# Ring of five 32 KB slots in place of nine of 16 KB, and the last output weights in three loads

## The chip, the cores and the metric

The kernel runs on one core of a Trainium2 chip. The metric is the device time of one execution in microseconds (us). Instructions run on TensorE (PE; its weight loads are listed as PEld), VectorE (DVE), ScalarE (ACT) and GpSimd (POOL). SyncE (SP) only issues transfers here; 16 DMA engines carry them out.

## The reference

One token passes through two blocks, and a gate mixes them. Block A is attention of 32 query heads over 4 groups of cached keys and values, 65536 positions of 128 numbers each; block B is a gated MLP. All inputs are bfloat16.

```python
q = (x @ wq).reshape(B, Sq, Hq, Dh)                  # 1 token, D = 1024, Hq = 32, Dh = 128
scores = einsum(q, k) * Dh ** -0.5                   # Hkv = 4, Sk = 65536, 8 heads share a group
a = (softmax(scores) @ v).reshape(1, Hq * Dh) @ wo
z = gelu(x @ w_in)                                   # D x 3584
z1, z2 = z[:1792], layernorm(z[1792:])
b = (z1 * (w_sp * z2 + b_sp)) @ w_out                # w_sp is 1 x 1
g = sigmoid((x * gate_w).sum())
out = g * a + (1 - g) * b
```

Keys and values are 4 x 65536 x 128 x 2 bytes each, 67.1 MB; with the weights the kernel reads 162.01 MB once.

## The kernel before

**Units.** A group's 65536 positions are cut in 8 units of 8192 positions (UK = 128 x 64). A unit of keys or values is one load of 2 MB: each of the 128 partitions receives 64 consecutive positions of 128 numbers, 16 KB in one run (`kv`). There are 32 key units and 32 value units.

**Ring.** All large loads go in one list, `stream`, in the order of their use: four loads of wq, then for each of the first eight steps a unit of keys, with one of four loads of w_in (steps 0 to 3) or one of two of w_out (steps 5 and 7), then keys and values in turn, and last four loads of wo. Load n goes to slot n modulo NS of a ring in SBUF (L323 issues it on SP). It waits until PE has finished with the load that held the slot before. The order in SP's queue is that of the list, and `issue` puts a load at the place of the program where its slot has been used up.

**Steps.** At step n PE works on key unit n and on value unit n - 9 (`k_piece`, `s_piece`, `pt_piece`, `pv_piece`).
- Keys: a unit goes in four pieces of 16 transposes (L388, 128 x 128 by an identity). Results lie in four PSUM banks; DVE (L396) or ACT (L393) copies them to one of NKTS key buffers. One piece later, four matmuls (L410) make scores from them.
- After the fourth piece DVE copies the unit's scores to one of NSC score buffers and takes their maximum (L415). When a group's eight units are done, its maximum is known.
- Values: ACT takes the exponentials of a unit's scores (L436), PE transposes them (L443), DVE copies them (L446), and 16 matmuls (L455) multiply them with the value unit. At the end of a group `out_piece` scales the sums and puts them into `ovec`.

**Around it.** At the start ACT issues four small loads: x, gate_w, w_sp and b_sp (`small`, L261). x and gate_w come as runs of two numbers, 4 bytes. PE's first instruction is a matmul for the gate (L348), which needs x and gate_w; the 256 matmuls with wq follow (L363). `win_piece` runs 56 matmuls (L503) for each of the four loads of w_in, with a weight operand whose 128 columns lie 7 numbers apart; after the fourth the mixer's chain of small operations runs, for which PE waits (L524, L529). `wout_piece` (L551) follows. At the end 32 matmuls for each load of wo (L598), one DVE addition (L604) and the output's transfer (L607).

Of the kernel before, what the change touches and what calls it, by code (L numbers as in the profile page):

```python
# [137 lines left out]
def bass_gated_mix__gqa_block_cached__mixer_gmlp__decode_kernel(  # L138
# [25 lines left out]
    TILES = 64  # L164
    UK = 128 * TILES
    NU = Sk // UK
    NS = 9
    SLOT = 8192
    NB = TILES // 8
    NKTS = 8  # L170
    NSC = 12
    QW = DO // 4
    SCALE = 1.0 / math.sqrt(Dh)
    GELU_C = 0.044715
# [52 lines left out]
    def slot(n):  # L227
        return ab("RING", SLOT, (n % NS) * SLOT)

# [14 lines left out]
    def B(i):  # L244
        return ("bank", i)
# [12 lines left out]
    def small(dst, src, key):  # L258
        def f(e):
            with nc.allow_non_contiguous_dma(reason="a few bytes"):  # L260
                return e.dma_start(dst, src)  # L261
        P("ACT", f, w=[key], dma=key)

    small(vw(xT, 0, [[2, 4], [1, 2]]), A_x[0, 0].rearrange("(i p k) -> p i k", i=4, k=2), "xT")
    small(vw(gw, 0, [[2, 4], [1, 2]]), gate_w.rearrange("(i p k) -> p i k", i=4, k=2), "gw")
    small(wb[:, 0:1], bass.AP(tensor=B_w_sp.tensor, offset=B_w_sp.offset, ap=[[0, 128], [1, 1]]), "wsp")
    small(wb[:, 1:2], bass.AP(tensor=B_b_sp.tensor, offset=B_b_sp.offset, ap=[[0, 128], [1, 1]]), "bsp")


    stream = []  # L270
    place = {}

    def load(key, src, n):
        place[key] = len(stream)
        stream.append((key, src, n))

    def rows(w, i, c):

# [1 line left out]

    WQ_N = HQ * Dh

    def kv(cache, g, u):
        return cache[0, g, UK * u:UK * (u + 1), :].rearrange("(p x) d -> p (x d)", p=128)

    KV = [(g, u) for g in range(G) for u in range(NU)]
    for i in range(4):
        load(("wq", i), rows(A_wq, i, 2), 2 * WQ_N)
    steps = []
    for n in range(NU):  # L290
        load(("k", n), kv(A_k_cache, *KV[n]), SLOT)
        aux = None
        if n < 4:
            load(("win", n), rows(B_w_in, n, 2), 2 * F)
            aux = ("win", n)
        elif n in (5, 7):
            i = (n - 5) // 2
            load(("wout", i), rows(B_w_out, i, 7), 7 * DO)
            aux = ("wout", i)
        steps.append((n, None, aux))  # L300
    total = G * NU
    for n in range(NU, total + NU + 1):
        k = n if n < total else None
        v = n - NU - 1
        if k is not None:
            load(("k", k), kv(A_k_cache, *KV[k]), SLOT)
        if v >= 0:
            load(("v", v), kv(A_v_cache, *KV[v]), SLOT)
        else:
            v = None  # L310
        steps.append((k, v, None))
    for i in range(4):
        load(("wo", i), rows(A_wo, i, 8), 8 * DO)

    issued = [0]

    def issue(upto):
        while issued[0] < min(upto, len(stream)):
            n = issued[0]
            assert n < NS or stream[n - NS][0] in used  # L320
            key, src, ln = stream[n]
            s = n % NS
            P("SP", lambda e, n=n, src=src, ln=ln: e.dma_start(slot(n)[:, 0:ln], src), w=[("slot", s)], dma="s%d" % s)  # L323
            issued[0] += 1

    used = set()

    def use(key):
        issue(place[key] + 1)
        used.add(key)  # L330
        return slot(place[key]), ("slot", place[key] % NS)

    issue(NS)

# [22 lines left out]
    for i in range(4):  # L357
        sl, key = use(("wq", i))

        def f(e, i=i, sl=sl):  # L360
            for k in range(2):
                for h in range(HQ):
                    ins = e.matmul(pf(OB)[:, h:h + 1], sl[:, WQ_N * k + 128 * h:WQ_N * k + 128 * (h + 1)],  # L363
                                   xT[:, 2 * i + k:2 * i + k + 1], start=(i == 0 and k == 0 and h == 0),
                                   stop=(i == 3 and k == 1), skip_group_check=True)
            return ins
        P("PE", f, r=["xT", key], w=[B(OB)])
        issue(place[("wq", i)] + NS + 1)
    for g in range(G):
        P("DVE", lambda e, g=g: e.tensor_copy(vw(qpad, 128 * g, [[40, 4], [1, 8]]),  # L370
                                              vw(pf(OB), 8 * g, [[0, 4], [1, 8]])),
# [6 lines left out]
    def k_piece(n, j):  # L378
        sl, key = use(("k", n))
        first = nbatch[0]  # L380
        for b in (2 * j, 2 * j + 1):
            i = nbatch[0]
            nbatch[0] += 1
            pb = KTB[i % 4]

            def tr(e, b=b, pb=pb):
                for t in range(8):
                    ins = e.transpose(pbf(pb)[:, 128 * t:128 * (t + 1)],  # L388
                                      sl[:, 128 * (8 * b + t):128 * (8 * b + t + 1)], idb)
                return ins  # L390
            P("PE", tr, r=["idb", key], w=[B(pb)])
            if b in (2, 5, 7):
                P("ACT", lambda e, i=i, pb=pb: e.activation(ktb(i), pbf(pb), ACTF.Copy),  # L393
                  w=[("kt", i % NKTS), B(pb)])
            else:
                P("DVE", lambda e, i=i, pb=pb: e.tensor_copy(ktb(i), pbf(pb)), w=[("kt", i % NKTS), B(pb)])  # L396
        if j == 3:
            issue(place[("k", n)] + NS + 1)
        pend.append((n, j, first))

    def s_piece():
# [46 lines left out]
    def pv_piece(n):  # L448
        g, u = KV[n]
        sl, key = use(("v", n))  # L450

        def f(e):
            for xi in range(4):
                for cg in range(4):
                    ins = e.matmul(pf(OB)[32 * cg:32 * (cg + 1), :],  # L455
                                   ptsb(n)[:, 128 * xi + 32 * cg:128 * xi + 32 * (cg + 1)],
                                   vw(sl, 128 * (4 * cg + xi), [[2048, 4], [1, 128]]),
                                   start=(u == 0 and xi == 0), stop=(u == NU - 1 and xi == 3),
                                   tile_position=(0, 32 * cg), skip_group_check=True)
            return ins  # L460
        P("PE", f, r=[("ptsb", n % 2), key], w=[B(OB)])
        issue(place[("v", n)] + NS + 1)
        if u == NU - 1:
            out_piece(g)

# [30 lines left out]
    def win_piece(i):  # L496
        sl, key = use(("win", i))

        def f(e):
            for k in range(2):  # L500
                for z in range(2 * FC):
                    c0 = F * k + FH * (z // FC) + 128 * 7 * (z % FC // 7) + z % 7
                    ins = e.matmul(pf(MB)[:, z:z + 1], vw(sl, c0, [[7, 128]]), xT[:, 2 * i + k:2 * i + k + 1],  # L503
                                   start=(i == 0 and k == 0 and z == 0), stop=(i == 3 and k == 1),
                                   skip_group_check=True)
            return ins
        P("PE", f, r=["xT", key], w=[B(MB)])
        issue(place[("win", i)] + NS + 1)
        if i == 3:
            mixer_piece()  # L510

# [33 lines left out]
    def wout_piece(i):  # L545
        sl, key = use(("wout", i))

        def f(e):
            for c in range(7):
                for q in range(4):  # L550
                    ins = e.matmul(pf(MB)[32 * q:32 * q + 1, 0:QW], yb[:, 7 * i + c:7 * i + c + 1],  # L551
                                   sl[:, DO * c + QW * q:DO * c + QW * (q + 1)],
                                   start=(i == 0 and c == 0), stop=(i == 1 and c == 6), tile_position=(0, 32 * q),
                                   skip_group_check=True)
            return ins
        P("PE", f, r=["yb", key], w=[B(MB)])
        issue(place[("wout", i)] + NS + 1)
        if i == 1:
            P("ACT", lambda e: e.activation(brow[0:97, :], pf(MB)[0:97, 0:QW], ACTF.Copy), w=["brow", B(MB)])

# [8 lines left out]
    for si, (k, v, aux) in enumerate(steps):  # L569
# [14 lines left out]
                pv_piece(v)  # L584
        if v is not None and v % NU == 0:
            weight_piece(v // NU)
        if aux is not None:
            (win_piece if aux[0] == "win" else wout_piece)(aux[1])


    FB = KTB[0]
    for i in range(4):
        sl, key = use(("wo", i))

        def f(e, i=i, sl=sl):
            for c in range(8):
                for q in range(4):
                    ins = e.matmul(pf(FB)[32 * q:32 * q + 1, 0:QW], ovec[:, 8 * i + c:8 * i + c + 1],  # L598
                                   sl[:, DO * c + QW * q:DO * c + QW * (q + 1)],
                                   start=(i == 0 and c == 0), stop=(i == 3 and c == 7), tile_position=(0, 32 * q),  # L600
                                   skip_group_check=True)
            return ins
        P("PE", f, r=[("ovec", i), key], w=[B(FB)])
    P("DVE", lambda e: e.tensor_tensor(orow[0:97, :], pf(FB)[0:97, 0:QW], brow[0:97, :], ALU.add),  # L604
      r=["brow"], w=["orow", B(FB)])
    osrc = bass.AP(tensor=arena, offset=OFF["OROW"], ap=[[32 * NA, 4], [1, QW]])
# [31 lines left out]
```

## Time and profile before

| | us |
|---|---|
| median of 8 runs (lowest, highest) | 395.24 (394.88, 395.69) |
| the profiled execution | 395.69 |
| its span, first to last instruction | 393.2 |
| PE busy | 275.0 (70%) |
| DVE busy | 160.3 (41%) |
| ACT busy | 124.3 (32%) |
| first matmul starts | 41.01 |
| last matmul of wo starts its group | 388.74 |

The span is read as 40 equal slices of 9.8 us. Each row of the second part of the profile gives an engine's busy share in tenths, and a last row the bytes moved per second. Queue q1 is SP's, with all large loads; q10 is ACT's, with the four small ones; q8 and q14 carry instructions. A wait is named after what ended it: "PE <- DMA" means that PE stood until a transfer had landed.

### The profile page before, as it was taken

Reading aid. Unit: us, or ns where it says so; the run is one execution under the profiler, and the core shown is the slowest. Engines: PE = TensorE matmul, PEld = TensorE weight load, DVE = VectorE, ACT = ScalarE, POOL = GpSimd, SP = SyncE. Lnnn points to the kernel's source line nnn. Section 1 sums busy time; section 2 is a strip of 40 time slices with the busy share of each in tenths; the row PEclk is TensorE's granted clock in tenths of the full one; section 3 lists DMA queues with packets and bytes.
Section 4 is the critical chain, followed back from the end, with each engine's and each line's share of the span. In section 5 each row is a group of like instructions: output and inputs, shape, how many; then the busy total and the mean of one; then the engine's idle time right before and its main releaser. Section 6 shows DMA issues by size and latency. Waiting matters only on the chain.

```text
span 393.2 us, 8544 instructions
## 1 busy us (share of the span) xinstructions
PE 275.0 (70%) x3902; PEld 194.6 (49%) x3902; DVE 160.3 (41%) x347; ACT 124.3 (32%) x171; POOL 1.5 (0%) x8
## 2 busy tenths in 40 slices
PE   0000699996998999997957687679767775644543
PEld 0000688885776666665645455457545553211121
DVE  2000044346666666676535345366434454200200
ACT  1000033333556555553614234235233334210000
POOL 1000000000000000000000000000000000000000
PEclk9999998986999999998989889689888898555555
DMA  8999999999999999999999999999999999999992
GB/s 315 405 418 422 421 428 431 427 422 424 425 422 430 423 430 425 427 427 426 425 427 427 427 425 423 425 427 428 428 430 427 424 428 423 430 424 425 432 395 89
DMA packets 12619, 162.55 MB, mean 413 GB/s; under 512 B 2596, under 2 KB 2600, under 8 KB 2600
## 3 DMA queue, kind: packets, MB, share of 16 engines
q1 hardware_dynamic: 11240, 162.01, 97.3%
q8 instruction: 30, 0.49, 0.5%
q10 hardware_dynamic: 1344, 0.00, 0.2%
q14 instruction: 5, 0.04, 0.0%
HBM read 162.01 MB, written 0.00 MB: 412 GB/s over the span
## 4 chain that ended last, share of the span: by engine, by line
DMA 60%; PE 30%; DVE 7%; ACT 1%; issue 1%; ACTq 0%; DVEq 0%
DMA arena<-in_A_k_cache_dram 30%; PE pb L388 16%; DMA arena<-in_A_wo_dram 11%; DMA arena<-in_gate_w_dram 10%; DMA arena<-in_A_v_cache_dram 10%; PE pb L410 5%; DVE arena L396 4%; PE pb L503 3%; PE pb L455 2%; PE pb L363 2%; DVE arena L415 2%; PE pb L443 1%; ACT arena L393 0%; PE pb L598 0%; PE pb L551 0%
## 5 line engine op out<-in xcount | busy, mean ns | idle before, releaser
L388 PE MATMUL pb<-arena 128*128 128x128 bf16 x2048 | 153.9, 235 | 27.7 <-DMA arena<-in_A_k_cache_dram 27.6
L388 PEld LDWEIGHTS pb<-arena 128*128 128x128 bf16 x2048 | 132.6, 106 | 56.1 <-DMA arena<-in_A_k_cache_dram 33.1
L396 DVE COPY arena<-pb 128x1024 bf16<-128x1024 bf16 x160 | 108.4, 690 | 110.5 <-PE pb L388 109.7
L393 ACT ACTIVATE arena<-pb 128x1024 bf16<-128x1024 bf16 x96 | 97.9, 1020 | 161.3 <-PE pb L388 161.3
L410 PE MATMUL pb<-arena 128*32 128x512 bf16 x512 | 54.8, 418 | 5.7 <-DVE arena L415 3.8
L455 PE MATMUL pb<-arena 128*32 128x512 bf16 x512 | 40.1, 441 | 19.4 <-DMA arena<-in_A_v_cache_dram 18.7
L455 PEld LDWEIGHTS pb<-arena 128*32 128x32 bf16 x512 | 14.2, 104 | 33.3 <-issue 22.5
L348 PE MATMUL pb<-arena 128*128 128x1 f32 x2 | 0.6, 361 | 41.0 <-DVE arena L347 41.0
L436 ACT ACTIVATE arena<-arena 128x512 bf16<-128x512 f32 x32 | 22.8, 713 | 16.3 <-PE pb L443 14.5
L446 DVE COPY arena<-pb 128x512 bf16<-128x512 bf16 x32 | 13.6, 424 | 29.7 <-PE pb L443 29.7
L410 PEld LDWEIGHTS pb<-arena 128*32 128x32 bf16 x512 | 13.3, 93 | 22.1 <-DVE arena L415 7.0
L415 DVE TENSOR_SCALAR_CACHE_REDUCE arena<-pb 128x512 f32<-128x512 f32 x32 | 21.8, 682 | 2.8 <-PE pb L410 2.8
L348 PEld LDWEIGHTS pb<-arena 128*128 128x128 f32 x2 | 0.5, 309 | 41.0 <-DVE arena L347 41.0
L346 DVE TENSOR_TENSOR arena<-arena 128x8 f32<-128x8 bf16 x1 | 0.2, 166 | 37.2 <-DMA arena<-in_gate_w_dram 37.2
L443 PE MATMUL pb<-arena 128*128 128x128 bf16 x128 | 15.1, 253 | 0.0
L443 PEld LDWEIGHTS pb<-arena 128*128 128x128 bf16 x128 | 8.9, 112 | 11.3 <-issue 11.3
L598 PE MATMUL pb<-arena 128*1 128x256 bf16 x128 | 7.5, 413 | 8.8 <-DMA arena<-in_A_wo_dram 8.8
L503 PEld LDWEIGHTS pb<-arena 128*128 128x128 bf16 x224 | 12.3, 153 | 0.9 <-issue 0.9
L503 PE MATMUL pb<-arena 128*128 128x1 bf16 x224 | 12.6, 192 | 0.0
L350 ACT ACTIVATE arena<-pb 128x1 f32<-128x1 f32 x1 | 0.2, 171 | 34.7 <-PE pb L348 34.7
L598 PEld LDWEIGHTS pb<-arena 128*1 128x1 bf16 x128 | 3.8, 115 | 12.2 <-DMA arena<-in_A_wo_dram 6.7
L363 PE MATMUL pb<-arena 128*128 128x1 bf16 x256 | 7.1, 165 | 1.5 <-issue 1.5
(78 smaller groups left out, 60.5 us busy)
## 6 DMA issues: line engine op xcount, KB each, us to landing
arena<-in_A_k_cache_dram SPq DMA_DIRECT2D x32, 2048.0 KB, 29.5
arena<-in_A_v_cache_dram SPq DMA_DIRECT2D x32, 2048.0 KB, 37.3
arena<-in_A_wq_dram SPq DMA_DIRECT2D x4, 2048.0 KB, 14.6
arena<-in_A_wo_dram SPq DMA_DIRECT2D x4, 2048.0 KB, 42.0
arena<-in_B_w_in_dram SPq DMA_DIRECT2D x4, 1792.0 KB, 22.6
arena<-in_B_w_out_dram SPq DMA_DIRECT2D x2, 1792.0 KB, 15.9
arena<-in_A_x_dram ACTq DMA_DIRECT2D x1, 2.0 KB, 22.3
arena<-in_gate_w_dram ACTq DMA_DIRECT2D x1, 2.0 KB, 39.3
```

Source lines behind the costliest of these rows:

```text
L363: ins = e.matmul(pf(OB)[:, h:h + 1], sl[:, WQ_N * k + 128 * h:WQ_N * k + 128 * (h + 1)], xT[:, 2 * i + k:2 * i + k + 1], start=(i == 0 and ...
L388: ins = e.transpose(pbf(pb)[:, 128 * t:128 * (t + 1)], sl[:, 128 * (8 * b + t):128 * (8 * b + t + 1)], idb)
L393: P("ACT", lambda e, i=i, pb=pb: e.activation(ktb(i), pbf(pb), ACTF.Copy), w=[("kt", i % NKTS), B(pb)])
L396: P("DVE", lambda e, i=i, pb=pb: e.tensor_copy(ktb(i), pbf(pb)), w=[("kt", i % NKTS), B(pb)])
L410: ins = e.matmul(pf(SCB)[32 * cg:32 * (cg + 1), :], qpad[:, 128 * g + 32 * j:128 * g + 32 * (j + 1)], src, start=(j == 0), stop=(j == 3), ...
L415: P("DVE", lambda e: e.tensor_scalar(scs(n), pf(SCB), 0.0, None, op0=ALU.add, op1=ALU.max, accum_out=maxc[:, n:n + 1]), w=[("sc", n % NSC) ...
L436: P("ACT", lambda e: e.activation(psb(n), scs(n), ACTF.Exp, bias=gcol(g, K_NB), scale=SCALE, accum_out=lp[:, n:n + 1]), r=[("sc", n % NSC) ...
L443: ins = e.transpose(pbf(PTB)[:, 128 * xi:128 * (xi + 1)], psb(n)[:, 128 * xi:128 * (xi + 1)], idb)
L446: P("DVE", lambda e: e.tensor_copy(ptsb(n), pbf(PTB)[:, 0:512]), w=[("ptsb", n % 2), B(PTB)])
L455: ins = e.matmul(pf(OB)[32 * cg:32 * (cg + 1), :], ptsb(n)[:, 128 * xi + 32 * cg:128 * xi + 32 * (cg + 1)], vw(sl, 128 * (4 * cg + xi), [[ ...
L503: ins = e.matmul(pf(MB)[:, z:z + 1], vw(sl, c0, [[7, 128]]), xT[:, 2 * i + k:2 * i + k + 1], start=(i == 0 and k == 0 and z == 0), stop=(i ...
L598: ins = e.matmul(pf(FB)[32 * q:32 * q + 1, 0:QW], ovec[:, 8 * i + c:8 * i + c + 1], sl[:, DO * c + QW * q:DO * c + QW * (q + 1)], start=(i ...
```

## The change

- The ring has five slots of 32 KB per partition in place of nine of 16 KB. A load brings two units: keys n and n + 1, values n and n + 1, two loads of wq or w_in, or both of w_out. A partition receives 128 consecutive positions of keys, 32 KB in one run (28 KB for w_in and w_out). The slot is free when PE has finished with the second unit (`done`).
- The rows of wq, w_in and w_out are dealt to the partitions in blocks of 4 and 14 in place of 2 and 7, and x and gate_w to match, in runs of 8 bytes.
- The weight operand of L503 has its columns 14 numbers apart in place of 7. The two w_in units of a load are used one after the other, after steps 1 and 3; both w_out units after step 6.
- wo comes in six loads: three of 2 MB as before, and the fourth in pieces of 4, 2 and 2 of its 8 rows per partition, with 16, 8 and 8 matmuls.
- Key buffers (NKTS) go from 8 to 6 and score buffers (NSC) from 12 to 10.

```diff
-    NS = 9
-    SLOT = 8192
+    NS = 5
+    SLOT = 16384
     NB = TILES // 8
-    NKTS = 8
-    NSC = 12
+    NKTS = 6
+    NSC = 10
...
-    small(vw(xT, 0, [[2, 4], [1, 2]]), A_x[0, 0].rearrange("(i p k) -> p i k", i=4, k=2), "xT")
-    small(vw(gw, 0, [[2, 4], [1, 2]]), gate_w.rearrange("(i p k) -> p i k", i=4, k=2), "gw")
+    small(vw(xT, 0, [[4, 2], [1, 4]]), A_x[0, 0].rearrange("(i p k) -> p i k", i=2, k=4), "xT")
+    small(vw(gw, 0, [[4, 2], [1, 4]]), gate_w.rearrange("(i p k) -> p i k", i=2, k=4), "gw")
...
+    def kv(cache, n):
+        g, u = KV[n]
+        return cache[0, g, UK * u:UK * (u + 2), :].rearrange("(p x) d -> p (x d)", p=128)
+
+    def pair(name, cache, n):
+        load([(name, n), (name, n + 1)], [(0, kv(cache, n))])
...
+    for i in range(0, 4, 2):
+        load([("wq", i), ("wq", i + 1)], [(0, rows(A_wq, i // 2, 4))])
     steps = []
     for n in range(NU):
+        if n % 2 == 0:
+            pair("k", A_k_cache, n)
+        aux = ()
+        if n in (1, 3):
+            load([("win", n - 1), ("win", n)], [(0, rows(B_w_in, n // 2, 4))])
+            aux = (("win", n - 1), ("win", n))
+        elif n == 5:
+            load([("wout", 0), ("wout", 1)], [(0, rows(B_w_out, 0, 14))])
+        elif n == 6:
+            aux = (("wout", 0), ("wout", 1))
...
+    WO = [(0, 0, 8), (1, 0, 8), (2, 0, 8), (3, 0, 4), (3, 4, 6), (3, 6, 8)]
+    for i, c0, c1 in WO:
+        load([("wo", i, c0)], [(0, rows(A_wo, i, 8)[:, DO * c0:DO * c1])])
...
+    def done(key):
+        n = place[key][0]
+        if key == stream[n][0][-1]:
+            issue(n + NS + 1)
...
-                    c0 = F * k + FH * (z // FC) + 128 * 7 * (z % FC // 7) + z % 7
-                    ins = e.matmul(pf(MB)[:, z:z + 1], vw(sl, c0, [[7, 128]]), xT[:, 2 * i + k:2 * i + k + 1],
+                    c0 = F * k + FH * (z // FC) + z % FC
+                    ins = e.matmul(pf(MB)[:, z:z + 1], vw(sl, c0, [[FC, 128]]), xT[:, 2 * i + k:2 * i + k + 1],
...
-    for i in range(4):
-        sl, key = use(("wo", i))
+    for i, c0, c1 in WO:
+        sl, key = use(("wo", i, c0))
...
+            for c in range(c0, c1):
                 for q in range(4):
+                    o = DO * (c - c0) + QW * q
...
+                                   sl[:, o:o + QW], start=(i == 0 and c == 0), stop=(i == 3 and c == 7),
```

More of the change, by code (lines that the diff above doesn't have):

```diff
@@ L271, in bass_gated_mix__gqa_block_cached__mixer_gmlp__decode_kernel, with load @@
     place = {}
-    def load(key, src, n):
-        place[key] = len(stream)
-        stream.append((key, src, n))
+    def load(keys, pieces):
+        for i, key in enumerate(keys):
+            place[key] = (len(stream), i)
+        stream.append((keys, pieces))
     def rows(w, i, c):
@@ L281, in bass_gated_mix__gqa_block_cached__mixer_gmlp__decode_kernel @@
     WQ_N = HQ * Dh
-    def kv(cache, g, u):
-        return cache[0, g, UK * u:UK * (u + 1), :].rearrange("(p x) d -> p (x d)", p=128)
+    def kv(cache, n):
[3 more added lines that the diff above has]
+        load([(name, n), (name, n + 1)], [(0, kv(cache, n))])
     KV = [(g, u) for g in range(G) for u in range(NU)]
-    for i in range(4):
-        load(("wq", i), rows(A_wq, i, 2), 2 * WQ_N)
+    total = G * NU
+    for i in range(0, 4, 2):
+        load([("wq", i), ("wq", i + 1)], [(0, rows(A_wq, i // 2, 4))])
     steps = []
     for n in range(NU):
[L291 to L299, printed above, removed]
+        if n % 2 == 0:
[8 more added lines that the diff above has]
+            aux = (("wout", 0), ("wout", 1))
         steps.append((n, None, aux))
-    total = G * NU
     for n in range(NU, total + NU + 1):
@@ L304, in bass_gated_mix__gqa_block_cached__mixer_gmlp__decode_kernel @@
         v = n - NU - 1
-        if k is not None:
-            load(("k", k), kv(A_k_cache, *KV[k]), SLOT)
+        if k is not None and k % 2 == 0:
+            pair("k", A_k_cache, k)
         if v >= 0:
-            load(("v", v), kv(A_v_cache, *KV[v]), SLOT)
+            if v % 2 == 0:
+                pair("v", A_v_cache, v)
         else:
             v = None
-        steps.append((k, v, None))
-    for i in range(4):
-        load(("wo", i), rows(A_wo, i, 8), 8 * DO)
+        steps.append((k, v, ()))
+    WO = [(0, 0, 8), (1, 0, 8), (2, 0, 8), (3, 0, 4), (3, 4, 6), (3, 6, 8)]
+    for i, c0, c1 in WO:
+        load([("wo", i, c0)], [(0, rows(A_wo, i, 8)[:, DO * c0:DO * c1])])
+    WIDTH = {"wq": 2 * WQ_N, "win": 2 * F, "wout": 7 * DO, "wo": 8 * DO, "k": UK, "v": UK}
     issued = [0]
+    used = set()
     def issue(upto):
@@ L319, in issue, with f @@
             n = issued[0]
-            assert n < NS or stream[n - NS][0] in used
-            key, src, ln = stream[n]
+            assert n < NS or all(k in used for k in stream[n - NS][0])
+            keys, pieces = stream[n]
             s = n % NS
-            P("SP", lambda e, n=n, src=src, ln=ln: e.dma_start(slot(n)[:, 0:ln], src), w=[("slot", s)], dma="s%d" % s)
+            def f(e, n=n, pieces=pieces):
+                for c0, src in pieces:
+                    ins = e.dma_start(slot(n)[:, c0:c0 + src.shape[1]], src)
+                return ins
+            P("SP", f, w=[("slot", s)], dma="s%d" % s)
             issued[0] += 1
-    used = set()
     def use(key):
-        issue(place[key] + 1)
+        n, i = place[key]
+        issue(n + 1)
         used.add(key)
-        return slot(place[key]), ("slot", place[key] % NS)
+        w = WIDTH[key[0]]
+        return slot(n)[:, i * w:(i + 1) * w], ("slot", n % NS)
+    def done(key):
+        n = place[key][0]
+        if key == stream[n][0][-1]:
+            issue(n + NS + 1)
     issue(NS)
@@ L367, in bass_gated_mix__gqa_block_cached__mixer_gmlp__decode_kernel @@
         P("PE", f, r=["xT", key], w=[B(OB)])
-        issue(place[("wq", i)] + NS + 1)
+        done(("wq", i))
     for g in range(G):
@@ L397, in k_piece @@
         if j == 3:
-            issue(place[("k", n)] + NS + 1)
+            done(("k", n))
         pend.append((n, j, first))
@@ L461, in pv_piece @@
         P("PE", f, r=[("ptsb", n % 2), key], w=[B(OB)])
-        issue(place[("v", n)] + NS + 1)
+        done(("v", n))
         if u == NU - 1:
@@ L507, in win_piece @@
         P("PE", f, r=["xT", key], w=[B(MB)])
-        issue(place[("win", i)] + NS + 1)
+        done(("win", i))
         if i == 3:
@@ L556, in wout_piece @@
         P("PE", f, r=["yb", key], w=[B(MB)])
-        issue(place[("wout", i)] + NS + 1)
+        done(("wout", i))
         if i == 1:
@@ L586, in bass_gated_mix__gqa_block_cached__mixer_gmlp__decode_kernel, with f @@
             weight_piece(v // NU)
-        if aux is not None:
-            (win_piece if aux[0] == "win" else wout_piece)(aux[1])
+        for a in aux:
+            (win_piece if a[0] == "win" else wout_piece)(a[1])
     FB = KTB[0]
-    for i in range(4):
-        sl, key = use(("wo", i))
-        def f(e, i=i, sl=sl):
-            for c in range(8):
+    for i, c0, c1 in WO:
+        sl, key = use(("wo", i, c0))
+        def f(e, i=i, sl=sl, c0=c0, c1=c1):
+            for c in range(c0, c1):
                 for q in range(4):
+                    o = DO * (c - c0) + QW * q
                     ins = e.matmul(pf(FB)[32 * q:32 * q + 1, 0:QW], ovec[:, 8 * i + c:8 * i + c + 1],
-                                   sl[:, DO * c + QW * q:DO * c + QW * (q + 1)],
-                                   start=(i == 0 and c == 0), stop=(i == 3 and c == 7), tile_position=(0, 32 * q),
-                                   skip_group_check=True)
+                                   sl[:, o:o + QW], start=(i == 0 and c == 0), stop=(i == 3 and c == 7),
+                                   tile_position=(0, 32 * q), skip_group_check=True)
             return ins
         P("PE", f, r=[("ovec", i), key], w=[B(FB)])
+        done(("wo", i, c0))
     P("DVE", lambda e: e.tensor_tensor(orow[0:97, :], pf(FB)[0:97, 0:QW], brow[0:97, :], ALU.add),
```

## The prediction

> **What bounds the kernel now.** I read the page from its second part down: slices, queues, then the waits, the stretches and the last microseconds.
>
> ```profile
> span 393.2 us, 8544 instructions
> DMA  8999999999999999999999999999999999999992
> GB/s 315 405 418 422 421 428 431 427 422 424 425 422 430 423 430 425 427 427 426 425 427 427 427 425 423 425 427 428 428 430 427 424 428 423 430 424 425 432 395 89
> q1 hardware_dynamic: 11240, 162.01, 97.3%
> q10 hardware_dynamic: 1344, 0.00, 0.2%
> ```
>
> The reader is to see that the DMA engines are full in every slice but the first and the last, and that one queue, q1 (SP's loads), is 97.3% of it. The rate is flat near 426 GB/s. q10 holds ACT's four small loads: 1344 packets in 0.2% of 16 x 393.2 us, so 9.4 ns for a packet of a few bytes.
>
> ```profile
> DMA to landing us min/median/max: 7.8/36.1/43.3
> PE pb L388 <- DMA arena<-in_A_k_cache_dram: 27.6, 12, 4.0
> PE pb L455 <- DMA arena<-in_A_v_cache_dram: 18.7, 9, 2.5
> SPq L323 <- PE pb L388: 221.7, 32, 10.5
> ```
>
> The shortest time from issue to landing is 7.8 us, while a 2 MB load alone takes 2097 KB / 426 GB/s = 4.92 us: no load was issued to an empty queue. PE waits for keys and values; SP waits for PE to free slots. So the time is bytes over rate, plus the start, plus what follows the last landing.
>
> The stretches (columns: PE, PEld, DVE, ACT and POOL busy, clock, DMA share, GB/s) show where PE has no slack:
>
> ```profile
> 42.00:50.00 8.00, 6.48 (x243) 6.42 (x241) 0.32 (x2) 0.00 (x0) 0.00 (x0) 1.00 1.02 423
> 50.00:88.00 38.00, 37.79 (x541) 31.84 (x538) 15.86 (x30) 12.28 (x12) 0.00 (x0) 0.91 1.00 425
> 160.00:250.00 90.00, 70.61 (x992) 49.79 (x988) 45.97 (x93) 36.80 (x51) 0.00 (x0) 0.92 1.01 426
> 250.00:340.00 90.00, 68.94 (x868) 48.01 (x872) 43.53 (x95) 32.58 (x50) 0.00 (x0) 0.82 1.01 426
> ```
>
> From 50 to 88 us PE is busy 37.79 of 38 us and works off a backlog; the ring hides that. From 160 us it idles a fifth. The tail, from the timeline:
>
> ```profile
> 388.74 1.87 PE L598 MATMUL pb<-arena 128*1 128x256 bf16 x32 [3.07 <-DMA arena<-in_A_wo_dram]
> 390.67 0.42 DVE L604 TENSOR_TENSOR arena<-pb,arena 97x256 bf16<-97x256 f32 x1 [15.52 <-PE pb L598]
> 391.12 0.65 SPq L607 DMA_DIRECT2D out_dram<-arena  x1
> ```
>
> The last 2 MB lands at 388.7, and its 32 matmuls (388.74 to 390.67, 1.9 us) stand on the path.
>
> **What the Trainium skill says.** "DMA: Bandwidth & Descriptors", section "Where 436 GB/s comes from", gives a ceiling of 435.2 GB/s; the trace's 426 is 98% of it, so the bytes can go hardly faster. Section "Why small descriptors are slow (HBM only)" of that page gives a fixed cost of some 3 cycles per packet; the trace before has nearly all its bytes in 14 and 16 KB packets and can't separate the two. Section "Queues, rings and completion order" says that an engine goes round its queues packet by packet: the trace agrees, since gate_w's few bytes took 39.3 us to land beside big packets. "SBUF — State Buffer", section "Door 1: The DMA port swizzle", says that SBUF is read in 16-byte lines and a crossing to a new line costs; used below.
>
> **The change, part by part.**
>
> *Packets of q1.* An engine gets 8 of a load's 128 rows. Before: (64 K/V + 4 wq + 4 win + 2 wout + 4 wo) x 8 = 624 packets per engine. After: 32 K/V, 2 wq, 2 win and 1 wout loads with rows of 28 or 32 KB, and six wo loads, 43 x 8 = 344. So 280 fewer. What is one worth? At 426 GB/s an engine needs 16384 / 26.62 = 615.4 ns for 16 KB, at the skill's ceiling 602.4. The excess of 13 ns is the most a packet can cost by itself; the skill's 3 cycles at that page's 850 MHz, an estimate of 3.5 ns, is my lower end. I take the middle, 8 ns: 280 x 8 = 2.2 us (1.0 to 3.6). It lies on the path, as q1 is never idle. A longer packet could also run slower, for which no row exists; I bound that loss by the spread of the middle slices (422 to 431 GB/s, 1% about their mean): 1% of 380 us, 4 us.
>
> *Completion packets.* 78 loads become 43; 35 fewer per engine at 9.4 ns: 0.3 us, on the path.
>
> *x and gate_w in runs of 8 bytes, not 4.* 512 fewer small packets, 32 per engine, at 9.4 ns: 0.3 us. Each waits for one big packet of the other queue: 64 x 0.6 us before, 32 x 1.2 us after. So gate_w lands at the same 40.5 us (1.24 + 39.26 in the chain of waits) within some 0.5, and PE starts near 41.5 us. wsp and bsp land later, by some 10 us; they are needed only by the mixer at 91 us.
>
> *The last output weights.* Now 16, 8 and 8 matmuls behind three landings. Eight take 1.9 x 8/32 = 0.5 us, so 1.4 us less after the last byte. wo piece 6 reuses the slot of wo piece 1, so it is issued only after that one's 32 matmuls, some 10 us after the last V pair lands, and its turn in the queue comes some 18 us after that landing: hidden by the 7 MB in between.
>
> *The ring.* Five slots of two units against nine of one. The danger is an empty queue in the stretch where PE has no slack. The first five loads are 20.4 MB; 16.5 MB are through at 42 us (403 GB/s over 1 to 42), the rest by 51.2. The next loads end at 59.9 (win), 69.7, 78.3 (wout), 88.2, 98.0 and 107.9 (first V). PE does the same work as before in another order: wq to 50, two keys, win twice (3.0 us each), two keys, win twice by 88.2, the mixer by 92.5, two keys by 104.9. Slots come free at about 45, 49, 63.7, 69.7, 82, 88 and 104.7; each must be before the queue runs out, at 51.2, 59.9, 69.7, 78.3, 88.2, 98.0 and 107.9. The smallest margin is the last: 3.2 us, some 2 to 3 after the time from issue to first byte. Later a pair of steps takes PE 2 x 6.7 = 13.4 us against 19.7 of transfer, and the margin grows. Cost 0, covered by queued loads. SP has 35 fewer issues of 0.33 us and nothing waits behind them.
>
> *Strided weights of win.* The 128 columns of L503 now lie 28 bytes apart, not 14. In the chain of waits:
>
> ```profile
> 41.59 5.89 PE pb L363 x221
> 56.93 3.08 PE pb L503 x56
> ```
>
> Contiguous weights take 5.89/221 = 26.7 ns a matmul, a stride of 14 bytes 55.0 ns. A stride of 14 bytes enters a new 16-byte line in 7 of 8 reads, 28 bytes in all 8: by lines (27 to 55 for 7/8) 59 ns, +0.9 us over 224 matmuls, inside the margin. If cost follows bytes, 110 ns: +12.3 us. Below nothing isn't likely. I take +0.9, hidden.
>
> *Smaller score and key buffers* (12 to 10, 8 to 6). The waits list has L396 and L393 waiting for L388 alone (109.7 and 161.3 us), never for L410, the reader of the key buffers. A score is overwritten ten units after it was made and read eight to nine after: still a whole step of 6.7 us. Cost 0.
>
> Sum: 2.2 + 0.3 + 0.3 + 1.4 = 4.2 us. The profiled execution took 395.69 us for a span of 393.2 (2.5 around it) and is the slowest of the eight; against it I expect a span of 389.0. Against the median, 395.24: **391.0 us**.
>
> **Rivals.**
> 1. *No gain per byte* (the rows are cut into 16 KB packets, or the excess is per byte): left are 0.3 + 0.3 + 1.4, less little: 393.3. For it: the rate is already 98% of the ceiling.
> 2. *The ring runs dry* in the win stage, because the wider stride slows L503. Place: the load of keys 10 and 11, freed when PE has done keys 4 and 5. It decides from about 3 us of delay, 13 ns per L503 matmul, and every us more is lost once for all; beyond 7.2 us (87 ns a matmul) the kernel is slower than before. At 110 ns: 12.3 - 3 - 4.2 = +5.1, 400.3 us. For it: the strided matmul already costs twice the contiguous one; against: one access per line is nearly reached at 14 bytes.
> 3. *Longer packets run slower*, or the granularity (PE starts on a pair only when both units are there) costs 2 to 4 us somewhere: about 395, no change.
>
> **How the numbers follow.** Forecast 0.63, rival 1 0.18, rival 2 0.13, rival 3 0.06. A measurement of this kernel can tell about 0.2% (0.8 us) from no change. Forecast and rival 1 are both faster, nearly all: 0.80; slower 0.14, same 0.06. The forecast's ends: 3.6 for packets gives 389.6, and a little more at the tail or the start 389.0; 1.0 gives 392.2; rival 1 with a loss of 1 us gives 394.3. Range 389.0 to 394.3.
>
> **What would show it.** Steps right: some 5,500 data packets on q1 (43 x 128) and the rate in the middle stretches near 430 to 432; no slice from the second to the last but one under 415; L598 after the last landing 0.5 us. Waits of PE for keys half as many and near 6 us each. Wrong: a slice below 400 between 90 and 120 us with L503 near 100 ns (rival 2); a middle rate still at 426 (rival 1); gate_w landing much later than 42 us; a shortest issue-to-landing time equal to a bare transfer of 9.8 us for a K or V pair.

## The result, and the profile after

The changed kernel takes 391.78 us (median of 11 runs, 390.64 to 392.77), the one before 395.19 us beside it. The ratio is 0.9913, with a 95% interval of 0.9904 to 0.9923: 3.4 us less (3.0 to 3.8). The profiled execution took 392.55 us with a span of 390.7 us, so it is 0.8 us above the median. The spans of its executions lie between 388.8 and 391.0 us; those of the kernel before, in all its runs beside the experiments, between 393.0 and 393.5. In the kernel after, L412 are the transposes, L434 the score matmuls, L387 those of wq, L527 those of w_in, L479 those of the values, L623 those of wo, and L339 issues the large loads.

The page, second and third part:

```profile
span 390.7 us, 8504 instructions
PEclk9999999595899999996899896968996889856555
DMA  8999999999989999999999999999999999999993
GB/s 322 429 429 436 421 417 439 428 425 428 401 324 428 441 435 428 436 424 434 424 428 424 434 428 436 428 424 431 434 434 429 434 429 434 429 428 429 408 420 149
q1 hardware_dynamic: 6200, 162.01, 97.1%
```

Two things are to be seen. The middle slices run a little above those of before. And the slices 10 and 11 (counted from 0: 97.7 to 117.2 us) fall to 401 and 324 GB/s. In these microseconds the DMA engines are not full; between its first and its last two slices, the kernel before has no slice under 405.

The same in stretches (busy time of PE, PEld, DVE, ACT and POOL, then the granted share of PE's full clock, DMA share, GB/s):

```profile
50.00:88.00 38.00, 36.92 (x523) 30.91 (x523) 15.77 (x30) 12.28 (x12) 0.00 (x0) 0.85 1.00 426
88.00:105.00 17.00, 13.87 (x171) 11.44 (x170) 9.02 (x30) 4.79 (x7) 0.00 (x0) 0.63 1.00 430
105.00:120.00 15.00, 14.37 (x249) 10.54 (x246) 9.60 (x18) 7.76 (x9) 0.00 (x0) 1.00 0.87 353
160.00:250.00 90.00, 69.95 (x972) 49.52 (x970) 44.33 (x88) 35.30 (x50) 0.00 (x0) 0.89 1.00 429
250.00:340.00 90.00, 67.43 (x914) 47.35 (x912) 44.59 (x95) 34.66 (x50) 0.00 (x0) 0.86 1.00 429
```

From 160 to 340 us the rate is 429 against 426. From 105 to 120 us the DMA share is 0.87, so 13% of 15 us, 2.0 us, went unused in this execution. PE is busy 14.37 of these 15 us: it isn't waiting, it is late. Over a longer stretch, first the kernel before and then the changed one:

```profile
88.00:125.00 37.00, 32.15 (x482) 24.15 (x480) 24.47 (x59) 18.62 (x22) 0.00 (x0) 0.91 1.01 428
```

```profile
88.00:125.00 37.00, 33.03 (x488) 25.71 (x487) 22.22 (x56) 15.40 (x17) 0.00 (x0) 0.83 0.95 400
```

SP's part of the timeline says what was late:

```profile
84.15 0.33 SPq L339 DMA_DIRECT2D arena<-in_A_k_cache_dram  x1
91.29 0.33 SPq L339 DMA_DIRECT2D arena<-in_A_v_cache_dram  x1
108.37 0.33 SPq L339 DMA_DIRECT2D arena<-in_A_k_cache_dram  x1
115.84 0.33 SPq L339 DMA_DIRECT2D arena<-in_A_v_cache_dram  x1
```

The third line is the load of keys 10 and 11. It was issued at 108.37 us, when PE had freed the slot of keys 4 and 5. The prediction let the queue run out at 107.9; in stretches of 1 us from 105 us on the trace has a DMA share of 1.17, 0.38, 0.30 and 0.00, so most engines ran out soon after 106.

The tail, from the timeline of the last microseconds:

```profile
387.60 0.60 PE L623 MATMUL pb<-arena 128*1 128x256 bf16 x8 [0.65 <-DMA arena<-in_A_wo_dram]
388.24 0.42 DVE L629 TENSOR_TENSOR arena<-pb,arena 97x256 bf16<-97x256 f32 x1 [11.42 <-PE pb L623]
388.69 0.63 SPq L632 DMA_DIRECT2D out_dram<-arena  x1
```

From the first matmul after the last landing to DVE's start it is now 388.24 - 387.60 = 0.64 us, against 390.67 - 388.74 = 1.93 before.

### The profile page after: what moved, and what is told of

Its sections match the earlier page's. It is cut to its first block, busy times and chain, and to the rows that moved or that the text cites. A ratio compares the mean times of both kernels' runs of the same rounds, so it can differ in the third digit from the quotient of the medians.

```text
span 390.7 us, 8504 instructions
## 1 busy us (share of the span) xinstructions
PE 275.0 (70%) x3902; PEld 194.3 (50%) x3902; DVE 160.2 (41%) x347; ACT 124.3 (32%) x171; POOL 1.5 (0%) x8
## 4 chain that ended last, share of the span: by engine, by line
DMA 52%; PE 37%; DVE 7%; issue 1%; ACT 1%; ACTq 0%; DVEq 0%
DMA arena<-in_A_k_cache_dram 31%; PE pb L412 19%; DMA arena<-in_gate_w_dram 10%; DMA arena<-in_A_v_cache_dram 9%; PE pb L434 6%; DVE arena L420 4%; PE pb L527 3%; PE pb L479 3%; DMA arena<-in_A_wo_dram 2%; PE pb L387 2%; DVE arena L439 2%; PE pb L467 1%; PE pb L623 1%; ACT arena L417 0%; PE pb L575 0%
## 5 line engine op out<-in xcount | busy, mean ns | idle before, releaser
L412 PE MATMUL pb<-arena 128*128 128x128 bf16 x2048 | 153.4, 235 | 32.7 <-DMA arena<-in_A_k_cache_dram 32.7
L412 PEld LDWEIGHTS pb<-arena 128*128 128x128 bf16 x2048 | 131.9, 106 | 61.1 <-DMA arena<-in_A_k_cache_dram 35.8
L420 DVE COPY arena<-pb 128x1024 bf16<-128x1024 bf16 x160 | 108.4, 689 | 112.0 <-PE pb L412 111.4
L417 ACT ACTIVATE arena<-pb 128x1024 bf16<-128x1024 bf16 x96 | 97.9, 1020 | 163.9 <-PE pb L412 163.9
L434 PE MATMUL pb<-arena 128*32 128x512 bf16 x512 | 54.8, 418 | 6.1 <-DVE arena L439 4.2
L479 PE MATMUL pb<-arena 128*32 128x512 bf16 x512 | 40.0, 441 | 14.2 <-DMA arena<-in_A_v_cache_dram 10.2
L479 PEld LDWEIGHTS pb<-arena 128*32 128x32 bf16 x512 | 14.0, 104 | 28.2 <-issue 13.4
L460 ACT ACTIVATE arena<-arena 128x512 bf16<-128x512 f32 x32 | 22.8, 713 | 14.2 <-PE pb L467 12.4
L434 PEld LDWEIGHTS pb<-arena 128*32 128x32 bf16 x512 | 13.3, 93 | 22.8 <-DVE arena L439 7.7
L467 PEld LDWEIGHTS pb<-arena 128*128 128x128 bf16 x128 | 8.6, 109 | 11.3 <-issue 10.5
L527 PEld LDWEIGHTS pb<-arena 128*128 128x128 bf16 x224 | 13.6, 159 | 0.5 <-issue 0.5
L527 PE MATMUL pb<-arena 128*128 128x1 bf16 x224 | 13.8, 198 | 0.0
L623 PE MATMUL pb<-arena 128*1 128x256 bf16 x128 | 7.7, 410 | 4.5 <-DMA arena<-in_A_wo_dram 4.4
L387 PE MATMUL pb<-arena 128*128 128x1 bf16 x256 | 7.1, 165 | 3.2 <-issue 3.2
L387 PEld LDWEIGHTS pb<-arena 128*128 128x128 bf16 x256 | 7.2, 105 | 3.2 <-issue 3.2
```

The lines of the kernel that those rows point to most:

```text
L412: ins = e.transpose(pbf(pb)[:, 128 * t:128 * (t + 1)], sl[:, 128 * (8 * b + t):128 * (8 * b + t + 1)], idb)
L434: ins = e.matmul(pf(SCB)[32 * cg:32 * (cg + 1), :], qpad[:, 128 * g + 32 * j:128 * g + 32 * (j + 1)], src, start=(j == 0), stop=(j == 3), ...
L460: P("ACT", lambda e: e.activation(psb(n), scs(n), ACTF.Exp, bias=gcol(g, K_NB), scale=SCALE, accum_out=lp[:, n:n + 1]), r=[("sc", n % NSC) ...
L467: ins = e.transpose(pbf(PTB)[:, 128 * xi:128 * (xi + 1)], psb(n)[:, 128 * xi:128 * (xi + 1)], idb)
L479: ins = e.matmul(pf(OB)[32 * cg:32 * (cg + 1), :], ptsb(n)[:, 128 * xi + 32 * cg:128 * xi + 32 * (cg + 1)], vw(sl, 128 * (4 * cg + xi), [[ ...
L527: ins = e.matmul(pf(MB)[:, z:z + 1], vw(sl, c0, [[FC, 128]]), xT[:, 2 * i + k:2 * i + k + 1], start=(i == 0 and k == 0 and z == 0), stop=( ...
```

## The experiments

The theory after the result: packets, completion packets, small packets and the tail give some 4 to 5 us, and a gap before keys 10 and 11 takes 1 to 2 us back. The rival: the packets give little, and there is no gap worth the name. All ratios below are against the kernel before.

**Where is PE late: the stride of w_in's weights (e2).** Hidden units are dealt as in the kernel before, with w_out's load to match:

```diff
-            load([("wout", 0), ("wout", 1)], [(0, rows(B_w_out, 0, 14))])
+            load([("wout", 0), ("wout", 1)], [(0, B_w_out.rearrange("(b p c) n -> p b (c n)", b=2, c=7))])
...
-                    c0 = F * k + FH * (z // FC) + z % FC
-                    ins = e.matmul(pf(MB)[:, z:z + 1], vw(sl, c0, [[FC, 128]]), xT[:, 2 * i + k:2 * i + k + 1],
+                    c0 = F * k + FH * (z // FC) + 128 * 7 * (z % FC // 7) + z % 7
+                    ins = e.matmul(pf(MB)[:, z:z + 1], vw(sl, c0, [[7, 128]]), xT[:, 2 * i + k:2 * i + k + 1],
```

> The changed kernel, with the weight columns of w_in 14 bytes apart as before (w_out's rows are dealt to match, in runs of 14 KB). Theory (the queue runs dry before keys 10 and 11 because PE is late there): 224 matmuls at 55 in place of 60 ns bring PE 1.1 to 1.4 us forward, and the gap shrinks by as much: 390.4 to 390.8 us. Rival (the slow slices are not a matter of PE being late): no change, 391.8.

Measured: 390.8 us, ratio 0.9885 (0.9873 to 0.9898), so 1.1 us less than the changed kernel (0.9913 - 0.9885, of 395). PE's timeline of the changed kernel, and then of this one:

```profile
64.16 6.88 PE L527 MATMUL pb<-arena 128*128 128x1 bf16 x112
84.38 6.88 PE L527 MATMUL pb<-arena 128*128 128x1 bf16 x112
```

```profile
64.19 6.13 PE L529 MATMUL pb<-arena 128*128 128x1 bf16 x112
82.65 6.13 PE L529 MATMUL pb<-arena 128*128 128x1 bf16 x112
```

The stride costs 0.75 us twice, 1.5 us. In this run the load of keys 10 and 11 goes out at 105.67 in place of 108.37 us, 2.7 us earlier. So 1.2 us of that are not the stride's: PE waits 0.3 us less among the matmuls of wq, and more of its transposes run at the full clock. Such differences also stand between executions of the same code: e4 (below), equal to the changed kernel up to wo, issues this load at 106.86. The stretch of the gap reads:

```profile
105.00:120.00 15.00, 14.58 (x253) 10.82 (x251) 9.18 (x17) 7.91 (x9) 0.00 (x0) 1.00 0.99 413
```

The DMA share is back to 0.99, though the rate, 413 GB/s, is still under its usual 430. The theory holds; the rival's "no change" lies outside the interval.

**What is a delay worth there (e9).** Each matmul of w_in gets a twin whose result nobody reads:

```diff
+                    e.matmul(pf(MB)[:, 32 + z:33 + z], vw(sl, c0, [[FC, 128]]), xT[:, 2 * i + k:2 * i + k + 1],
+                             start=False, stop=(i == 3 and k == 1), skip_group_check=True)
                     ins = e.matmul(pf(MB)[:, z:z + 1], vw(sl, c0, [[FC, 128]]), xT[:, 2 * i + k:2 * i + k + 1],
```

> The changed kernel, with each of the 224 matmuls of w_in preceded by a twin into unused columns of the same bank: PE is 224 x 60 ns = 13.5 us later when it frees keys 4 and 5. Theory (the ring has no margin left there, so every us of delay before keys 10 and 11 is an idle us of the queue and is never won back): 12 to 13.5 us more than the changed kernel, 403.8 to 405.3 us, with the slices from 90 to 120 us far under 400 GB/s. Rival (the ring absorbs several us and the gap in the changed kernel is chance): 5 us more or less than that, under 397 us.

Measured: 405.04 us, ratio 1.0252 (1.0229 to 1.0274), 13.3 us above the changed kernel. In the profiled execution PE's wait among the matmuls of wq is 1.1 us shorter (2.08 in place of 3.19 us), so of 13.5 us of added work 12.4 reach the load of keys 10 and 11, which goes out at 120.75 in place of 108.37 us. The span grows by as much, from 390.7 to 403.1 us. SP's line, and the page's rates:

```profile
120.75 0.33 SPq L339 DMA_DIRECT2D arena<-in_A_k_cache_dram  x1
```

```profile
GB/s 348 433 416 416 415 415 442 408 308 415 265 158 382 441 422 428 437 429 418 439 432 421 434 437 421 429 424 437 431 428 431 426 438 421 431 436 424 418 420 159
```

The slices 8, 10 and 11 fall to 308, 265 and 158: the queue is now empty three times, before 90, before 104 and before 121 us. From 125 us on the rate is 430, as in e2: a microsecond in which the queue is empty is not won back. The ring had no slack left, and the rival, with 5 us or less, is out.

**Without PE's late start (e3, e7, e5).** e3 issues x and gate_w on SP's queue ahead of all large loads; e7 puts them behind the first wq load; e5 does the latter in the kernel before.

```diff
-        P("ACT", f, w=[key], dma=key)
+        P("SP" if key in ("xT", "gw") else "ACT", f, w=[key], dma=key)     # e3
...
+    issue(1)                                                               # e7, e5: first load, then x and gate_w on SP
+    small(..., "xT", "SP")
+    small(..., "gw", "SP")
     issue(NS)
```

> The changed kernel, with x and gate_w issued on SP's queue ahead of the large loads in place of on ACT's. PE can then start when the first wq load lands, at some 13 us, in place of 41. Theory (the gap is PE's late start and backlog): the gap goes, 2 to 3 us less, and the large loads start 0.5 to 1 us later: 389.3 to 390.3 us, and no slice under 415 GB/s between the first and the tail. Rival (the slow slices have another cause): 391.8 plus the later start, 392.3 to 392.8.

> The changed kernel, with x and gate_w on SP's queue behind the first wq load. Unlike with x and gate_w ahead of all, no large load starts later. Theory (the gap before keys 10 and 11 costs 1.9 us, and in the run with x and gate_w ahead the later start of the loads, 3.5 in place of 1.7 us, ate just that): 389.6 to 390.2 us. Rival (the gap costs nothing, the time is set elsewhere): 391.7 us as in that run.

> The kernel before, with x and gate_w issued on SP's queue behind the first wq load in place of on ACT's: PE starts at some 8 us in place of 41, and no large load starts later. Theory (before, the queue was never empty, so an early PE is worth nothing but fewer mixed-in packets): within 0.4 us of the kernel before, 394.8 to 395.3. Rival (an early start gains by itself, for instance by less work left at the end): 393.3 us, the 1.9 us that the gap is put at.

Measured: e3 391.7 us, 0.9906 (0.9892 to 0.9920); e7 391.35 us, 0.9900 (0.9888 to 0.9913); e5 396.37 us, 1.0025 (1.0016 to 1.0035). The gap closes in both e3 and e7: no slice of e7 from the third to the tail is under 415 GB/s. But the time falls by 0.1 and 0.4 us only: both missed their forecasts. So did the control e5: its profile has no gap, yet it is 1.0 us slower (0.6 to 1.4). Small loads in SP's queue have a price. In e7 it is paid in the first 20 us. Here e7, then the changed kernel:

```profile
0.00:20.00 20.00, 4.00 (x130) 3.91 (x130) 3.18 (x14) 1.45 (x2) 1.45 (x8) 1.00 0.93 361
```

```profile
0.00:20.00 20.00, 0.00 (x0) 0.00 (x0) 2.38 (x9) 1.28 (x1) 1.45 (x8) 1.00 0.95 388
```

27 GB/s less over 20 us are 540 KB; from 20 to 42 us e7 runs at 428 against 419 GB/s and wins 198 KB back. The 342 KB left are 0.8 us at 428 GB/s. So e7 puts the gap at 0.4 + 0.8 = 1.2 us; e2 says 1.1. The 1.0 us of e5 can't be carried over to e7: its small runs are half as long and so twice as many, and its spans scatter from 393.2 to 395.6 us, for which no run shows the reason.

**What is a long packet worth (e1, e8).** Keys and values in two runs of 16 KB per partition, same loads, same ring; e1 from the changed kernel, e8 from e7.

```diff
-        return cache[0, g, UK * u:UK * (u + 2), :].rearrange("(p x) d -> p (x d)", p=128)
+        return cache[0, g, UK * u:UK * (u + 2), :].rearrange("(b p x) d -> p b (x d)", b=2, p=128)
```

> The changed kernel, with the two units of a key or value load as two runs of 16 KB per partition in place of one of 32 KB: same ring, same number of loads, packets of 16 KB again. Theory (a long packet saves some 10 to 13 ns, and 2 to 3 us are lost in a gap before keys 10 and 11): 256 packets more per engine cost 2.6 to 3.3 us; the slower queue gives up to 1 us of the gap back: 393.7 to 394.9 us. Rival (packet size hardly matters, the gain of the change comes from the tail and the fewer small packets, and there is no gap worth the name): under 1 us more, 391.8 to 392.7.

> As the run before this one, with keys and values in two runs of 16 KB per partition: packets of 16 KB in a ring that never runs dry. Theory (a long packet saves 13 ns, and the run with 16 KB rows showed only 1.4 us because PE started earlier there and the gap closed): 256 x 13 ns = 3.3 us above the kernel with x and gate_w second, 393.0 to 393.5 us. Rival (the packet saves only what that run showed): 1.4 us above it, 391.3 us.

Measured: e1 393.18 us, 0.9944 (0.9932 to 0.9956), 1.4 us above the changed kernel, between the theory's and the rival's numbers. e8 393.65 us, 0.9958 (0.9946 to 0.9971), 2.3 us above e7 (0.6 to 0.7 either way, from the two intervals). e8 is the clean one: neither it nor e7 has a gap. e1 mixes two things, since the chain of waits shows its start moved:

```profile
1.22 31.94 DMA arena<-in_gate_w_dram
34.26 5.89 PE pb L389 x221
```

Beside packets half as long gate_w lands at 33.2 us in place of 40.5, PE starts 7 us earlier, and the gap is gone. So e1's 1.4 us fit 2.3 us of packets less about a microsecond of gap. 2.3 us for 256 packets per engine are 9 ns a packet (6 to 12 by the interval). Both forecasts that took up to 13 ns were too high: e1 stayed below its own, and e8 lies just above (393.65 against 393.0 to 393.5) only since e7, from which it counts, came out over a microsecond high.

**The tail (e4, e10).** e4 loads the last wo unit in one piece again; e10 starts from e2 and halves the last quarter.

```diff
-    WO = [(0, 0, 8), (1, 0, 8), (2, 0, 8), (3, 0, 4), (3, 4, 6), (3, 6, 8)]
+    WO = [(i, 0, 8) for i in range(4)]                                                   # e4
+    WO = [(0, 0, 8), (1, 0, 8), (2, 0, 8), (3, 0, 4), (3, 4, 6), (3, 6, 7), (3, 7, 8)]   # e10, with e2's edit
```

> The changed kernel, with the fourth load of wo in one piece of 2 MB again. Both theories: the last landing has 32 matmuls behind it, 1.9 in place of 0.6 us; two completion packets and 16 data packets per engine fewer give 0.15 us back: 1.1 to 1.3 us more, 392.9 to 393.1 us. If the tail were covered by something else: no change.

> The kernel with the columns 14 bytes apart, and the last output weights in four pieces, a half, a quarter and two eighths of the 2 MB: 4 matmuls after the last landing in place of 8. Theory (matmuls after the last landing stand on the path, some 0.06 us each with a fixed part): 0.2 us less, 390.5 us. Rival (a landing so small has a fixed price that eats it): 390.8 us or a little more.

Measured: e4 392.92 us, 0.9943 (0.9922 to 0.9963), 1.1 us above the changed kernel, as expected but with a wide interval. e10 390.73 us, 0.9894 (0.9876 to 0.9911): no difference from e2 can be told. Its last four matmuls take 0.44 us where the changed kernel's eight take 0.64:

```profile
385.99 0.38 PE L625 MATMUL pb<-arena 128*1 128x256 bf16 x4 [0.25 <-DMA arena<-in_A_wo_dram]
386.43 0.42 DVE L631 TENSOR_TENSOR arena<-pb,arena 97x256 bf16<-97x256 f32 x1 [11.11 <-PE pb L625]
```

Cutting by half no longer halves the time, and 0.2 us is below what five runs tell.

**The smaller buffers (e6).** The kernel before with the new numbers of key and score buffers:

```diff
-    NKTS = 8
-    NSC = 12
+    NKTS = 6
+    NSC = 10
```

> The kernel before, with 6 key buffers and 10 score buffers in place of 8 and 12. The prediction put this at 0: 395.2 us within 0.3. If the buffers are what PE or the copies wait for in the stretch from 50 to 110 us, PE is later there; before has 3 us or more of margin in the queue, so it would show in the trace as L410 in the waits of L396 or L393, and in the time only beyond that.

Measured: 395.74 us, ratio 1.0006 (0.9998 to 1.0015). The median lies outside the 0.3 us named, but the interval takes in no change and the spans, 393.1 to 393.4 us, are those of the kernel before: no cost that can be told. L396 and L393 wait for L388 alone, and in the changed kernel the copies (L420, L417) wait for the transposes (L412) alone, never for the score matmuls (L434).

**The version to keep** is e2: the changed kernel with the columns of w_in 14 bytes apart, 390.8 us, 1.1% below the kernel before and 0.3% below the changed one.

## Why the prediction was right or wrong

The forecast was 391.0 us, the result 391.78, inside the range and on the side given. The measured gain is 3.4 us, the forecast 4.2. That it came so near is in part luck: the start gave more than its term, and the ring, put at nothing, took more than a microsecond back.

- *Packets of q1, 2.2 us for 280 at 8 ns.* Right. e8 against e7 gives 9 ns, 2.5 us for 280. Neither end of the range (3.5 and 13 ns) was the price, and rival 1 (no gain per byte) is out: the stretches from 160 us on run at 429 in place of 426, though not at the 430 to 432 named. With that rival 3 is out too: the longer packets don't run slower, and from 125 us on no stretch shows a loss to the coarser grain. The fixed cost in the Trainium skill's page "DMA: Bandwidth & Descriptors", section "Why small descriptors are slow (HBM only)", 3 cycles a packet, an estimate of 3.5 ns at that page's 850 MHz, is smaller than what these runs show for a packet of a whole row.
- *Completion packets and x/gate_w, 0.3 us each.* Not tested apart. For x and gate_w the traces give more. The first 20 us of the kernel before:

```profile
0.00:20.00 20.00, 0.00 (x0) 0.00 (x0) 2.38 (x9) 1.28 (x1) 1.45 (x8) 1.00 0.92 364
```

  The changed kernel runs at 388 there (above), and both at 419 from 20 to 42 us. 24 GB/s over 20 us are 480 KB, 1.1 us. In 42 us an engine has some 32 large packets fewer (17 MB in packets of 32 in place of 16 KB), 0.3 us at 9 ns; an estimate from these figures; some 0.8 us are left. The small loads are the likely saver, but no run tests that. The parts are then 2.5 + 0.3 + 0.8 + 1.2 = 4.8 us, and less 1.1 to 1.2 for the gap 3.6 to 3.7, within the measured 3.0 to 3.8.
- *The start.* gate_w lands at 1.24 + 39.24 = 40.5 us, as forecast, since half as many small packets each wait for one twice as long; e1, with large packets half as long, has it at 33.2 us.
- *The tail, 1.4 us.* 1.3 us in the trace, 1.1 us by e4.
- *The smaller buffers, 0.* Right, by e6.
- *The ring, cost 0.* This step failed. The place was right: the load of keys 10 and 11, with a margin of 3.2 us, was named as the smallest. But PE freed keys 4 and 5 at 108.37, not 104.7. In the kernel before, the same work freed the slot of key unit 5 at 104.75:

```profile
104.75 0.33 SPq L323 DMA_DIRECT2D arena<-in_A_v_cache_dram  x1
```

  PE's timelines split the 3.6 us between the two into three terms:
  - The first transposes start at 51.59 in place of 49.94 us, 1.7 us later. PE waits for nothing that the trace shows ("issue") among the matmuls of wq, 3.19 us in place of 1.52. This was not foreseen at all.
  - From there to the mixer's first matmul (93.45 and 90.49 us) PE takes 41.86 in place of 40.55 us, 1.3 us more. The stride is 1.5 us by e2, where 0.9 was forecast (59 ns a matmul; 6.81/112 = 60.8 in the chain of waits); the rest is 0.2 us shorter.
  - From the mixer to the freed slot it takes 14.92 in place of 14.26 us, 0.7 us more. PE's granted clock from 88 to 105 us is 0.63 in place of 0.80. 16 transposes take 1.07 us where it is 1.00 and 1.87 us where it is 0.50.

  The queue, for its part, ran out about a microsecond before the 107.9 of the forecast, which counted on the pace of the kernel before; the first 42 us had carried 1.1 us more than there. So the margin was eaten from both ends. The sign that was named for an empty queue, a landing 9.8 us after its issue, is too strict: keys 10 and 11 landed 13.7 us after theirs, though the engines stood idle from 108 to 109 us.

The chains of waits, the kernel before and then the changed one, have the first term:

```profile
47.49 1.52 issue
```

```profile
41.58 5.89 PE pb L387 x221
47.47 3.19 issue
50.66 1.07 PE pb L387 x35
```

Its cause stays open. One candidate is that PE's instructions come by DMA too (queue q8) and stand behind packets twice as long. e1, with 16 KB packets of keys and values beside 32 KB ones of wq, has 2.23 us; but e9, with packets as long as in the changed kernel, has 2.08, and e4 3.51.

The wait and the clock differ between executions of the same code (e4 against the changed kernel: 3.51 and 3.19 us; 40.55 and 41.86 us from the first transposes to the mixer). With slack in the ring this stays hidden; without, it goes into the time. That fits the spans: they lie within 0.5 us in the kernel before and in e1, e3, e7 and e8, which have no gap, but spread over 2.2 us in the changed kernel, 2.7 in e4 and 1.8 in e9. Only e5 spreads (2.4 us) without a gap in its profile.

- *Rival 2* had the right mechanism and the right law: from the end of the margin on each microsecond counts once, as e9 shows, 12.4 us in the load and 12.4 in the span. Only its price was below what it needed: 61 ns a matmul, where 68 (55 and its 13) would have emptied the queue alone. So the outcome was the forecast with a small piece of this rival in it, which the sum left at nothing: three delays of 0.7 to 1.7 us, each of them below the margin of 3 us, add up to more than it.

## What to carry to other kernels

When transfers bound a kernel, a deeper or coarser ring is judged at the stage where the consumer is slowest, and its margin is a sum: list every delay of that stage, those of the change itself and those that a longer packet causes elsewhere, before calling the cost zero. Longer rows still pay in a queue that is full at 426 GB/s, some 9 ns for each packet saved, but coarser slots take the slack that hid the consumer's late work. A delay before an issue to an empty queue is lost in full, and no later stage wins it back.

## What the runs showed of the hardware

- A packet costs some 9 ns beside its bytes (e8 against e7: 2.3 us for 256 per engine, rows of 16 KB against 32 KB; 6 to 12 ns).
- A small load beside a stream of large ones on another queue lands after about as many large packets as there are small ones up to its end per engine (x and gate_w before: 64 of 0.615 us are 39.4): 39.3 us with 4-byte runs and 16 KB packets, 39.2 us with half as many runs and 32 KB packets. With half as many runs and 16 KB packets for keys, 31.9 us.
- A matmul of 128 x 128 weights with one column takes 26.7 ns with contiguous weight columns, 54.2 to 55.0 with columns 14 bytes apart, 60.8 with columns 28 bytes apart.
- 16 transposes take 1.07 us at a granted clock of 1.00 and 1.87 us at 0.50.
- x and gate_w in the queue of the large loads itself cost 1.0 us (e5; 0.6 to 1.4), though they are 4 KB; in e7, in runs twice as long, 0.8 us by its rates.
